# A linear-attention and two-MoE kernel: the diagonals of recurrence step 1 from a second set of scores, and conversion steps in other places

## The chip, the cores and the metric

The kernel runs on one core of a Trainium2 chip. A core has five engines with a queue of instructions each: TensorE (PE: matmuls; PEld: its weight loads), VectorE (DVE), ScalarE (ACT), GpSimd (POOL) and SyncE (SP), which here issues all transfers between memory and the core. Each engine runs its own queue in order and waits where data of another engine is due. The metric is the device time of one execution in microseconds.

## The reference

The inputs are r, k, v (4 batches, 8 heads, 768 positions, head size 48), a decay w and a bonus u for each head and channel, and the weights of two gated blocks. First comes a linear-attention recurrence for each batch and head:

```python
for t in range(S):
    cur = np.einsum('bhd,bhe->bhde', u[None] * kt, vt)
    y[:, :, t] = np.einsum('bhd,bhde->bhe', rt, state + cur)
    state = w[None, :, :, None] * state + np.einsum('bhd,bhe->bhde', kt, vt)
```

Its output, laid out as 3072 tokens of 384 features, goes through `(x @ w_a) * (x @ w_b) @ w_out` (1536 hidden features), and that through `((x @ w1) * (x @ w2)) @ w3 @ w_out` (1024 hidden features). Most weights arrive as 64-bit floats.

## The kernel before, in words

**Recurrence.** The 768 positions are cut into 6 steps of 128. A step and a batch make a unit: units 0 to 3 are step 0, 4 to 7 are step 1, and so on to 23. In a unit the decay is folded into scaled copies of r and k (`prep_r`, `prep_k`, lines 349 to 356: products with the tables tr and tk). `scores` (line 382) multiplies the scaled k with the scaled r into two PSUM tiles "at", one for the even and one for the odd heads; there are two such buffers (pool ps_at). `a_evac` (line 387) copies them to SBUF with the strictly causal mask applied. The diagonal of the scores needs the bonus u and no decay. Units 4 and later compute it apart: `prep_d` (line 358) multiplies r, u and k in their natural layout on GpSimd in two products and sums each head on VectorE into dg, and `a_diag` (line 395) copies dg into the diagonal under the mask ident. Units 0 to 3 have it from a second set of scores with k scaled by u, read from PSUM by `diag_0` (line 402). `y_mm` (line 410) multiplies the state and then the scores into the output tile, `y_evac` (line 447) splits the output into a high and a low part (fp32r, two matmul operands), `s_mm`, `s_decay` and `s_upd` (lines 468 to 500) update the state. The output and the state's increment take the two "at" buffers again.

**Weights.** The class Stream (line 56) takes 27 jobs for the first block, in this order: wab0, wab1, the first part of w_out, wab2, wab3, the second part of w_out, wab4, wab5, the third part of w_out, with three jobs each. A job loads 512 KB of 64-bit floats (line 86; four staging buffers, so a load waits for ScalarE to be done with the job four before it), turns them into 32-bit floats on VectorE (`begin`, lines 101, 117 and 120), casts the high part on ScalarE (`cast`, line 133) and subtracts it on VectorE for the low part (`finish`, line 154). `step` finishes one job and begins the next; `split` forces the jobs that a matmul is about to read.

**First block.** For each tile of 128 hidden features two groups of nine matmuls (line 631: three products of high and low parts, three slices of the depth) fill PSUM tiles "ab"; ScalarE copies one (g, line 650), VectorE multiplies it with the other (line 656), ScalarE casts the product (gh, line 657), VectorE takes its low part (gl, line 662). `m_mm` (lines 684 to 686) multiplies with w_out, two tiles later. The run for step 0 is cut after six tiles (SPLIT), so that the second run, for step 1, can follow.

**Order.** The program writes the order of each queue out by hand. `merge` (line 537) lays three lists into each other: main (the tile groups), side (the recurrence slots of the next step, eight for a unit) and late (conversion steps). In the first run, late spreads 12 or 13 steps evenly.

Of the kernel before, what the change touches and what calls it, by code (L numbers as in the profile page):

```python
# [7 lines left out]
F32 = mybir.dt.float32  # L8
# [12 lines left out]
C = 128  # L21
# [19 lines left out]
STEPS = (1, 1, 1, 0)  # L41
# [5 lines left out]
PRE = 3  # L47

END_0 = 4
LATE = 3  # L50
# [126 lines left out]
def rwkv_moe_kernel(ctx, tc, rkT, nat, wu, wab, wout, w12, w3T, wo2, r_in, k_in, v_in, w_in, u_in, out):  # L177
# [7 lines left out]
    def flat(ap):  # L185
        return ap.rearrange("p a b -> p (a b)")

    with tc.manual_schedule():
# [153 lines left out]
        nc.vector.tensor_tensor(out=wC, in0=pos[:, :, HALF:], in1=pos[:, :, HALF:], op=ALU.mult)  # L342
        s_t = [att.tile([112, NP, 112], F32, name=f"s{b}", bufs=1) for b in range(B)]
# [3 lines left out]
        kf_t, pr_t, y3_t = {}, {}, {}  # L347
# [34 lines left out]
        def scores(u):  # L382
            for x in range(2):
                at_ps[u, x] = ps_at.tile([128, NP, C], F32, name="at")
            scores_f([at_ps[u, x] for x in range(2)], flat(rf_t[u]), kf_t.pop(u))
# [9 lines left out]
        def a_diag(u, hf):  # L395
            d = d_t[u].rearrange("p (q x) -> p x q", x=2)[:, hf, :]
            nc.vector.copy_predicated(
                out=a_t[u][:, 4 * hf:4 * hf + 4, :],
                mask=ident.bitcast(I32).rearrange("p (o n) -> p o n", o=1).to_broadcast([128, 4, C]),
                data=d.rearrange("p (h o) -> p h o", o=1).to_broadcast([128, 4, C]))  # L400

# [100 lines left out]
        def prep_slots(u):  # L502
            return [
                lambda: (prep_r(u, nc.vector), prep_k(u, nc.vector)),
                lambda: prep_d(u, 0),
                lambda: prep_d(u, 1),
                lambda: prep_d(u, 2),
            ]

        def unit_slots(u):  # L510
# [7 lines left out]

            return [
# [72 lines left out]
        for u in range(B):  # L592
# [9 lines left out]
            y_0_evac(u)  # L602
            later_loads(u)
# [9 lines left out]
            for _ in range(STEPS[u]):  # L613
                step()
# [3 lines left out]
        step()  # L618
        for u in range(S_NOW, B):
            k_nat(u)  # L620
        for f in prep_slots(B)[:PRE]:
            f()
        for _ in range(TAIL - 1):
            step()
# [130 lines left out]
        for n, (q, tiles, c) in enumerate(runs):  # L755
# [8 lines left out]
            if n == 0:  # L764
                side = [lambda u=u: (s_mm(u), s_upd(u)) for u in range(S_NOW, B)] + prep_slots(B)[PRE:] + side
            if n == 0:
                late = [step] * (wo_ready[1] - st.begun)
            if n == 1:
                late = [step] * (len(st.jobs) - st.begun + 2)
                late += [lambda: None] * (len(late) // LATE)  # L770
# [359 lines left out]
```

## Time and profile before

| what | before |
|---|---|
| median of 3 runs | 918.27 us (917.95 to 923.23) |
| the profiled execution | 921.02 us, its span 919.2 us |
| mean granted TensorE clock | 0.984 |
| TensorE busy | 889.4 us (97%) |
| VectorE busy | 449.9 us (49%) |
| ScalarE busy | 325.2 us (35%) |
| GpSimd busy | 106.9 us (12%) |

The span goes from the first to the last instruction; the profiled execution's own time is 1.8 us longer, and it is 2.7 us over the median of the runs. The granted clock is the share of full speed that TensorE's clock had in a stretch: 1.0 is 2.4 GHz, 0.5 is 1.2 GHz. A busy time is an average over parts of the program that have different limits, so the table says little of the first 116 us, in which the recurrence's first steps, the conversions and the first tiles run side by side.

### The profile page before, as it was taken

The page shows a single profiled execution, that of the slowest core. Times are in us where ns is not written, and L with a number is a line of the kernel's source. Part 1 is how long each engine was busy: PE and PEld are TensorE (multiplying, and loading weights), DVE is VectorE, ACT ScalarE, POOL GpSimd, SP SyncE. Part 2 cuts the span into 40 slices and gives each one's busy share as a digit, 9 for nine tenths or more (in the row PEclk, how much of TensorE's full clock was granted, in tenths as well). Part 3 has the DMA queues.
Part 4 walks back from the last instruction along what each step waited for, and adds up shares of the span by engine and source line. Part 5 has one row for each costly group of instructions (what it writes and reads, how often), then busy time and mean ns, then how long its engine had stood idle before and what let it go on. Part 6 is the DMA issues. An engine that isn't in the chain of part 4 may idle for free.

```text
span 919.2 us, 12479 instructions
## 1 busy us (share of the span) xinstructions
PE 889.4 (97%) x4962; PEld 754.2 (82%) x4962; DVE 449.9 (49%) x762; ACT 325.2 (35%) x737; POOL 106.9 (12%) x104
## 2 busy tenths in 40 slices
PE   8877999999999999999999999999999999999997
PEld 7665788888888888888888888899988888888886
DVE  8998876356343333433332889566222222223212
ACT  3554565332222232222112778564322222222211
POOL 2204200036033213211100000000000000000000
PEclk9798899999999999999999999999999999999999
DMA  8654531024131221122103555352010101000001
GB/s 263 193 160 138 135 118 63 1 79 154 30 101 46 63 68 59 47 63 81 47 1 109 165 156 172 109 176 71 12 58 11 47 24 47 24 35 1 35 0 38
DMA packets 26065, 73.56 MB, mean 80 GB/s; under 512 B 3152, under 2 KB 7376, under 8 KB 26000
## 3 DMA queue, kind: packets, MB, share of 16 engines
q1 hardware_dynamic: 26000, 72.70, 26.1%
q8 instruction: 41, 0.67, 0.3%
q14 instruction: 24, 0.20, 0.1%
HBM read 61.28 MB, written 9.44 MB: 77 GB/s over the span
## 4 chain that ended last, share of the span: by engine, by line
PE 90%; DVE 6%; issue 1%; DMA 1%; ACT 1%; SPq 0%
PE ab L631 52%; PE m L684 5%; PE m L686 5%; PE m L685 5%; PE at L798 4%; PE o L822 3%; PE o L823 3%; PE o L821 3%; PE at L420 2%; PE at L380 2%; PE at L416 2%; DVE cvt L117 1%; DMA rk<-in_rkT_dram 1%; PE at L823 1%; PE at L821 1%
## 5 line engine op out<-in xcount | busy, mean ns | idle before, releaser
L656 DVE TENSOR_TENSOR ab<-g,ab 128x512 f32<-128x512 f32 x120 | 83.5, 696 | 305.2 <-PE ab L631 272.8
L631 PE MATMUL ab<-xt,w12h 128*128 128x512 f32 x576 | 177.4, 389 | 0.0
L650 ACT COPY g<-ab 128x512 f32<-128x512 f32 x120 | 70.4, 587 | 264.0 <-PE ab L631 263.9
L657 ACT CAST gh<-ab 128x512 fp32r<-128x512 f32 x120 | 70.5, 588 | 253.5 <-DVE ab L656 253.5
L631 PEld LDWEIGHTS ab<-xt,w12h 128*128 128x128 f32 x576 | 107.5, 188 | 18.8
L662 DVE TENSOR_TENSOR gl<-ab,gh 128x512 fp32r<-128x512 f32 x120 | 83.0, 691 | 61.5 <-ACT gh L657 60.8
L631 PE MATMUL ab<-xt,w12l 128*128 128x512 f32 x288 | 112.0, 389 | 0.0
L684 PE MATMUL m<-gh,woh 128*128 128x512 f32 x216 | 85.5, 396 | 0.4 <-ACT woh L133 0.4
L686 PE MATMUL m<-gh,wol 128*128 128x512 f32 x216 | 84.3, 390 | 0.8 <-DVE wol L154 0.8
L685 PE MATMUL m<-gl,woh 128*128 128x512 f32 x216 | 84.3, 390 | 0.0
L631 PEld LDWEIGHTS ab<-xt,w12l 128*128 128x128 f32 x288 | 54.1, 188 | 11.3
L352 POOL TENSOR_TENSOR rk<-rk,tr 112x512 f32<-112x512 f32 x16 | 20.7, 1294 | 281.5 <-DMA rk<-in_rkT_dram 140.3
L631 PE MATMUL ab<-xt,wab0h 128*128 128x512 f32 x144 | 48.0, 415 | 3.1 <-DVE xt L445 2.5
L684 PEld LDWEIGHTS m<-gh,woh 128*128 128x128 f32 x216 | 40.5, 188 | 10.2 <-ACT woh L133 0.8
L686 PEld LDWEIGHTS m<-gh,wol 128*128 128x128 f32 x216 | 40.5, 188 | 9.8 <-DVE wol L154 1.2
L685 PEld LDWEIGHTS m<-gl,woh 128*128 128x128 f32 x216 | 40.6, 188 | 8.3
L631 PE MATMUL ab<-xt,wab1h 128*128 128x512 f32 x144 | 46.9, 408 | 0.0
L631 PE MATMUL ab<-xt,wab4h 128*128 128x512 f32 x144 | 45.5, 397 | 0.0
L631 PE MATMUL ab<-xt,wab3h 128*128 128x512 f32 x144 | 45.5, 397 | 0.0
L631 PE MATMUL ab<-xt,wab2h 128*128 128x512 f32 x144 | 45.4, 397 | 0.0
L631 PE MATMUL ab<-xt,wab5h 128*128 128x512 f32 x144 | 45.0, 394 | 0.0
L117 DVE SCALAR_TENSOR_TENSOR cvt<-stg_t,cvt 128x512 int32<-128x512 int32 x61 | 44.6, 731 | 0.3
(275 smaller groups left out, 1582.2 us busy)
## 6 DMA issues: line engine op xcount, KB each, us to landing
natt<-in_nat_dram SPq DMA_DIRECT2D x20, 576.0 KB, 5.0
rk<-in_rkT_dram SPq DMA_DIRECT2D x24, 448.0 KB, 3.8
stg_t<-in_wab_dram SPq DMA_DIRECT2D x18, 512.0 KB, 4.0
stg_t<-in_w3T_dram SPq DMA_DIRECT2D x16, 512.0 KB, 3.9
stg_t<-in_w_dram SPq DMA_DIRECT2D x12, 512.0 KB, 3.7
stg_t<-in_wout_dram SPq DMA_DIRECT2D x9, 512.0 KB, 3.6
m_d<-m_sb SPq DMA_DIRECT2D x18, 256.0 KB, 3.2
stg_t<-m_d SPq DMA_DIRECT2D x18, 256.0 KB, 2.7
```

The lines of the kernel that those rows point to most:

```text
L117: nc.vector.scalar_tensor_tensor(out=f, in0=w[:, :, 1], scalar=-0x40000000, in1=f, op0=ALU.bitwise_and, op1=ALU.bitwise_or)
L631: mm(ps, lhsT=w[i][:, k, cs], rhs=x[:, j, k, :], start=(n == 0), stop=(n == 3 * KD - 1))
L650: nc.scalar.copy(out=t["g"], in_=t["a"])
L656: nc.vector.tensor_tensor(out=t["b"], in0=g, in1=t["b"], op=ALU.mult)
L657: nc.scalar.copy(out=gh, in_=t["b"])
L662: nc.vector.tensor_tensor(out=gl, in0=t["b"], in1=gh, op=ALU.subtract)
L684: mm(m_ps[q][k], lhsT=wh[:, j, cs], rhs=gh, start=first, stop=False)
L685: mm(m_ps[q][k], lhsT=wh[:, j, cs], rhs=gl, start=False, stop=False)
L686: mm(m_ps[q][k], lhsT=wl[:, j, cs], rhs=gh, start=False, stop=last)
L798: mm(f_ps[i], lhsT=w3_t[i][a][:, g, :], rhs=wo2_t[g // 4][b][:, g % 4, :], start=(n == 0), stop=(n == 3 * NF2 - 1))
L821: mm(o_ps[q][b], lhsT=ph[:, cs], rhs=wh, start=(f == 0), stop=False)
L823: mm(o_ps[q][b], lhsT=pl[:, cs], rhs=wh, start=False, stop=(f == NF2 - 1))
```

## The change

Units 4 to 7 (step 1) no longer use `prep_d`, `a_diag` and dg. A vector uw = u * w (clipped w) is made once. `prep_u` scales the already scaled k of a unit with uw on ScalarE into a tile ku (four activations), and `scores_u` multiplies ku with the scaled r into two more "at" tiles, whose diagonals `diag_0` copies. The decay exponents of the scaled r and k of one position differ by one factor of w, so the product with u * w gives the diagonal without decay. Unit 8 keeps its `prep_d`, in the slots of unit 7.

The conversion steps of the first run are no longer spread by the list late: there is one in the slot of a unit's scores, one in the slot of its `y_mm`, and four at the end of the run. In step 0, steps go ahead of the later loads, and finish, cast and begin are called one by one. In the second run every second place of late holds a step. The order of the jobs is the same.

```diff
--- before.py
+++ after.py
@@ -38,16 +38,13 @@
 
 WARM, WARM_0 = 10, 6
 
-STEPS = (1, 1, 1, 0)
 TAIL = 3
 
 S_NOW = 2
 
 SPLIT = 6
-PRE = 3
 
 END_0 = 4
-LATE = 3
 N_OK = 2 * 128 * N64 + 112 * NP
 
 EXP_LO, EXP_HI = 2.0 ** -15 * 1.125, 2.0 ** 16 * 1.8749
@@ -340,11 +337,13 @@
         nc.vector.tensor_copy(out=tk, in_=tr[:, :, ::-1])
         wC = const.tile([112, NP, 1], F32, name="wC")
         nc.vector.tensor_tensor(out=wC, in0=pos[:, :, HALF:], in1=pos[:, :, HALF:], op=ALU.mult)
+        uw = wc
+        nc.vector.tensor_tensor(out=uw, in0=ut, in1=wc, op=ALU.mult)
         s_t = [att.tile([112, NP, 112], F32, name=f"s{b}", bufs=1) for b in range(B)]
 
         rf_t, d_t, a_t, kn_t, at_ps, xt = {}, {}, {}, {}, {}, {}
 
-        kf_t, pr_t, y3_t = {}, {}, {}
+        kf_t, ku_t, pr_t, y3_t = {}, {}, {}, {}
 
         def prep_r(u, eng):
             r = rk_t[u][:, 0, :]
@@ -382,7 +381,7 @@
         def scores(u):
             for x in range(2):
                 at_ps[u, x] = ps_at.tile([128, NP, C], F32, name="at")
-            scores_f([at_ps[u, x] for x in range(2)], flat(rf_t[u]), kf_t.pop(u))
+            scores_f([at_ps[u, x] for x in range(2)], flat(rf_t[u]), kf_t[u])
 
         def a_evac(u, hf):
             if hf == 0:
@@ -398,6 +397,18 @@
                 out=a_t[u][:, 4 * hf:4 * hf + 4, :],
                 mask=ident.bitcast(I32).rearrange("p (o n) -> p o n", o=1).to_broadcast([128, 4, C]),
                 data=d.rearrange("p (h o) -> p h o", o=1).to_broadcast([128, 4, C]))
+
+        def prep_u(u):
+
+            ku_t[u] = att.tile([112, NP * C], F32, tag="m_part", name="ku", bufs=1)
+            for p in range(NP):
+                s = slice(p * C, (p + 1) * C)
+                nc.scalar.activation(out=ku_t[u][:, s], in_=kf_t[u][:, s], func=ACTF.Copy, scale=uw[:, p:p + 1])
+
+        def scores_u(u):
+            for x in range(2):
+                at_ps["d", u, x] = ps_at.tile([128, NP, C], F32, name="at")
+            scores_f([at_ps["d", u, x] for x in range(2)], flat(rf_t[u]), ku_t.pop(u))
 
         def diag_0(u):
 
@@ -502,9 +513,7 @@
         def prep_slots(u):
             return [
                 lambda: (prep_r(u, nc.vector), prep_k(u, nc.vector)),
-                lambda: prep_d(u, 0),
-                lambda: prep_d(u, 1),
-                lambda: prep_d(u, 2),
+                lambda: prep_u(u),
             ]
 
         def unit_slots(u):
@@ -516,6 +525,18 @@
                 if nxt:
                     f(n, *a)
 
+
+            if u < 2 * B:
+                return [
+                    lambda: (scores(u), after(prep_r, pool), step()),
+                    lambda: (a_evac(u, 0), a_evac(u, 1), after(prep_k, pool)),
+                    lambda: (scores_u(u), k_nat(u)),
+                    lambda: (diag_0(u), n < 2 * B and prep_u(n), n == 2 * B and prep_d(n, 0)),
+                    lambda: (y_mm(u), s_mm(u), step()),
+                    lambda: (load_rk(u + 2), load_nat(u + 2), y_evac(u), (u + 1) % B == 0 and y_shuffle(u // B),
+                             s_decay(u), n == 2 * B and prep_d(n, 1)),
+                    lambda: (s_upd(u), n == 2 * B and prep_d(n, 2)),
+                ]
             return [
                 lambda: (scores(u), after(prep_r, pool)),
                 lambda: (a_evac(u, 0), a_evac(u, 1), after(prep_k, pool)),
@@ -600,6 +621,11 @@
                 both_a(u + 1)
                 diag_0(u + 1)
             y_0_evac(u)
+            if u < 2:
+                step()
+            elif u == 2:
+                st.finish()
+                st.cast()
             later_loads(u)
             if u == 2:
                 tn_ps = ps_m.tile([128, NP, 112], F32, tag="m0", name="tn_ps")
@@ -610,17 +636,18 @@
                     nc.scalar.copy(out=tnat[:, :, x, :], in_=tn_ps[:, :, a:e])
                 for b in range(S_NOW):
                     k_nat(b)
-            for _ in range(STEPS[u]):
-                step()
+                st.finish()
         for u in range(S_NOW):
             s_mm(u)
             s_upd(u)
-        step()
+        st.begin()
+        st.cast()
         for u in range(S_NOW, B):
             k_nat(u)
-        for f in prep_slots(B)[:PRE]:
+        st.finish()
+        for f in prep_slots(B):
             f()
-        for _ in range(TAIL - 1):
+        for _ in range(TAIL):
             step()
 
 
@@ -762,12 +789,12 @@
                     main.append(m_slot(*lag.pop(0)))
             side = step_slots(c) if c else []
             if n == 0:
-                side = [lambda u=u: (s_mm(u), s_upd(u)) for u in range(S_NOW, B)] + prep_slots(B)[PRE:] + side
+                side = [lambda u=u: (s_mm(u), s_upd(u)) for u in range(S_NOW, B)] + side
             if n == 0:
-                late = [step] * (wo_ready[1] - st.begun)
+                late = [lambda: None] * (len(main) - END_0) + [step] * END_0
             if n == 1:
-                late = [step] * (len(st.jobs) - st.begun + 2)
-                late += [lambda: None] * (len(late) // LATE)
+                late = [step] * 2 + [step, lambda: None] * (len(st.jobs) - st.begun)
+                late += [lambda: None] * (len(main) - len(late))
             if q == NB - 1:
                 for i in range(4):
                     add_w12(i)
```

The order on two engines, before and then changed. VectorE, from the state update of unit 4 (s) to the diagonal of unit 5 (a_sc); cvt is a conversion, wol the low half of w_out's first part, gl a low half of the gated product:

```order
L498 TENSOR_TENSOR s_168<-at,s_168 48x4x48 x2
L366 TENSOR_REDUCE dg<-pr 128x8
L656 TENSOR_TENSOR ab<-g,ab 128x512
L154 TENSOR_TENSOR wol_617<-cvt,woh_616 128x512
L117 SCALAR_TENSOR_TENSOR cvt<-stg_t,cvt 128x512
L101 TENSOR_SCALAR cvt<-stg_t 128x512
L120 SCALAR_TENSOR_TENSOR cvt<-stg_t,cvt 128x512
L662 TENSOR_TENSOR gl<-ab,gh 128x512
L352 TENSOR_TENSOR rk<-rk,tr 112x512
L391 TENSOR_TENSOR a_sc<-at,mask 128x512 x2
L356 TENSOR_TENSOR rk<-rk,tk 112x512
L397 COPY_PREDICATED a_sc<-ident,dg 128x512 x2
```

```order
L509 TENSOR_TENSOR s_169<-at,s_169 48x4x48 x2
L351 TENSOR_TENSOR rk<-rk,tr 112x512
L151 TENSOR_TENSOR wol_629<-cvt,woh_628 128x512
L114 SCALAR_TENSOR_TENSOR cvt<-stg_t,cvt 128x512
L98 TENSOR_SCALAR cvt<-stg_t 128x512
L117 SCALAR_TENSOR_TENSOR cvt<-stg_t,cvt 128x512
L683 TENSOR_TENSOR ab<-g,ab 128x512
L689 TENSOR_TENSOR gl<-ab,gh 128x512
L390 TENSOR_TENSOR a_sc<-at,mask 128x512 x2
L355 TENSOR_TENSOR rk<-rk,tk 112x512
L372 TENSOR_TENSOR kn<-natt,tnat 128x384
L416 COPY_PREDICATED a_sc<-ident,at 128x512 x2
```

The reduction dg is gone; the r product of unit 6 (rk with tr) stands directly behind the state update, and the low half and the conversion stand ahead of the gated product; the natural k product (kn) and the key product are now between the masks and the diagonal, which reads "at" in place of dg.

SyncE, from the natural k of step 0 (k_96) to the load of w_out's first part; stg_t are the conversions' loads, rk and natt the loads of units 4 and 5:

```order
L291 DMA k_96<-in_nat_dram 128x384 x4
L86 DMA stg_t<-in_wab_dram 128x512 x2
L214 DMA rk<-in_rkT_dram 112x1024
L294 DMA u_bc<-in_u_dram 128x384
L223 DMA natt<-in_nat_dram 128x1152
L86 DMA stg_t<-in_wab_dram 128x512
L214 DMA rk<-in_rkT_dram 112x1024
L223 DMA natt<-in_nat_dram 128x1152
L86 DMA stg_t<-in_wout_dram 128x512 x3
```

```order
L288 DMA k_96<-in_nat_dram 128x384 x4
L83 DMA stg_t<-in_wab_dram 128x512 x2
L211 DMA rk<-in_rkT_dram 112x1024
L291 DMA u_bc<-in_u_dram 128x384
L220 DMA natt<-in_nat_dram 128x1152
L211 DMA rk<-in_rkT_dram 112x1024
L220 DMA natt<-in_nat_dram 128x1152
L83 DMA stg_t<-in_wout_dram 128x512 x3
```

The single load of wab between units 4 and 5 now stands ahead of unit 4's loads (the fourth one has moved ahead of k_96, so two remain behind it). On TensorE, the new 8 scores stand behind nine matmuls after the first 8 in units 5 to 7, and directly behind them in unit 4.

## Rows read from the trace of the kernel before

**Rows 1.** stretches: us, busy PE PEld DVE ACT POOL, granted clock, DMA, GB/s

```profile
0.00:28.30 28.30, 24.16 (x264) 21.36 (x264) 24.36 (x51) 10.46 (x29) 6.36 (x19) 0.94 0.86 259
...
28.30:99.99 71.69, 54.01 (x400) 42.38 (x397) 62.15 (x107) 37.70 (x101) 17.32 (x13) 0.83 0.51 153
...
50.00:53.20 3.20, 3.18 (x33) 2.67 (x33) 3.17 (x6) 2.02 (x8) 0.00 (x0) 0.50 0.80 196
...
116.09:919.20 803.11, 796.28 (x4240) 678.80 (x4238) 347.47 (x584) 267.07 (x585) 76.68 (x67) 1.00 0.22 66
```

**Rows 2.** TensorE's waits: us in total, times, longest

```profile
PE ab L631 <- DVE wab2l L154: 5.8, 2, 3.6
...
PE at L420 <- DVE a_sc L397: 4.2, 3, 2.8
...
PE at L380 <- DVE s L498: 3.1, 1, 3.1
```

**Rows 3.** timeline, TensorE: start us, us, engine, line, operation, idle before

```profile
57.51 1.16 PE L380 MATMUL at<-rk 48*128 48x128 f32 x16
...
58.60 0.73 PE L631 MATMUL ab<-xt,wab1h 128*128 128x512 f32 x2
...
60.78 1.04 PE L416 MATMUL at<-rk,s 112*112 112x128 f32 x8
...
70.85 2.04 PE L380 MATMUL at<-rk 48*128 48x128 f32 x14 [3.15 <-DVE s L498]
...
80.00 1.08 PE L420 MATMUL at<-a_sc,natt 128*48 128x128 f32 x16
...
114.40 0.50 PE L686 MATMUL m<-gh,wol 128*128 128x512 f32 x1 [0.76 <-DVE wol L154]
```

**Rows 4.** timeline, VectorE

```profile
25.40 1.34 DVE L405 COPY_PREDICATED a<-ident,d_ps 128x512 f32<-128x512 int32 x2
...
29.17 1.49 DVE L117 SCALAR_TENSOR_TENSOR cvt<-stg_t,cvt 128x512 int32<-128x512 int32 x1
...
33.39 0.68 DVE L117 SCALAR_TENSOR_TENSOR cvt<-stg_t,cvt 128x512 int32<-128x512 int32 x1
...
34.93 1.02 DVE L373 TENSOR_TENSOR k<-k,tnat 128x384 f32<-128x384 f32 x2
...
41.35 0.55 DVE L366 TENSOR_REDUCE dg<-pr 128x8 f32<-128x384 f32 x1
...
49.24 1.35 DVE L397 COPY_PREDICATED a_sc<-ident,dg 128x512 f32<-128x512 int32 x2
...
54.42 0.72 DVE L498 TENSOR_TENSOR s<-at,s 48x192 f32<-48x192 f32 x2 [0.36 <-ACT s L488]
...
99.27 0.72 DVE L498 TENSOR_TENSOR s<-at,s 48x192 f32<-48x192 f32 x2 [0.36 <-ACT s L488]
...
103.53 2.49 DVE L101 TENSOR_SCALAR cvt<-stg_t 128x512 int32<-128x512 int32 x1
...
113.67 0.68 DVE L154 TENSOR_TENSOR wol<-cvt,woh 128x512 fp32r<-128x512 f32 x1
```

**Rows 5.** groups by line, VectorE, 28.3-100 us: count, busy us, mean ns

```profile
L356 DVE TENSOR_TENSOR rk<-rk,tk 112x512 f32<-112x512 f32 x4 | 4.0, 1002 | 0.0
...
L352 DVE TENSOR_TENSOR rk<-rk,tr 112x512 f32<-112x512 f32 x4 | 2.7, 683 | 0.0
```

**Rows 6.** groups by line, GpSimd, 28.3 to 85 us

```profile
L361 POOL TENSOR_TENSOR pr<-natt,u_bc 128x384 f32<-128x384 f32 x4 | 6.6, 1654 | 45.4 <-DMA natt<-in_nat_dram 25.3 <-DVE dg L366 20.1
...
L363 POOL TENSOR_TENSOR pr<-pr,natt 128x384 f32<-128x384 f32 x4 | 4.3, 1078 | 0.3
```

**Rows 7.** timeline, ScalarE

```profile
98.01 1.23 ACT L488 ACTIVATE s<-s,wC 112x112 f32<-112x112 f32 x4
```

**Rows 8.** DMA issues at 51.85 and 61.85 us: KB, us from issue to landing

```profile
rk<-in_rkT_dram SPq DMA_DIRECT2D x1, 448.0 KB, 6.3
...
rk<-in_rkT_dram SPq DMA_DIRECT2D x1, 448.0 KB, 3.5
```

## The prediction

> **What bounds the kernel now.** I read the busy time by stretches first. From 116.1 us to the end TensorE works 796.28 of 803.11 us at the full granted clock; from 28.3 to 100.0 us (the recurrence's step 1 and the first feature tiles) it works 54.01 of 71.69 us at a mean granted clock of 0.83, and there VectorE is the busiest, 62.15 of 71.69 [rows 1]. The change edits only this head, so whatever it brings is a shift of the moment at which TensorE leaves it. Then TensorE's waits: those of weight are for VectorE, 5.8 us for the low half of a converted weight (wab2l), 4.2 us for the masked scores a_sc, 3.1 us for the state update s [rows 2]. The timeline shows what a wait costs beside its own length: the scores' 16 matmul records take 1.16 us, yet 14 of them take 2.04 us after the wait of 3.15 us [rows 3], and the granted clock is 0.50 (1.2 GHz) in the 3.2 us behind the wait of 2.8 us [rows 1, 2]. So the reader is to see a head in which VectorE's queue sets the pace and TensorE's clock falls after each longer wait. The head's last gate is the low half of w_out's second part: TensorE waits for it up to 114.40 us [rows 3]; VectorE starts it at 113.67 us, 14.4 us after the last unit's state update at 99.27 us [rows 4].
>
> **What the change removes.** For units 4 to 7 the products on GpSimd and their sum on VectorE go. The sums are four reductions of 0.55 us, 2.2 us of VectorE's queue [rows 4]. The eight products (6.6 + 4.3 = 10.9 us on GpSimd, [rows 6]) ran beside VectorE and stretched it: the conversion's L117 took 1.49 us at 29.17 us where 0.68 us is usual [rows 4], 0.8 us more, and the instruction behind it as much; the key product L356 takes 1.00 us on average and its twin L352 0.68, 4 x 0.32 = 1.3 us [rows 5]. That is 2.9 us. Together VectorE's queue gets 5.1 us shorter.
>
> The Trainium skill, page "SBUF — State Buffer", has a stronger rule: a VectorE instruction with two SBUF inputs and a GpSimd instruction that reads SBUF share a port pair, held exclusively for a whole instruction, so that the second blocks fully. By that rule up to all 10.9 us of the products could come back, where the rows give 2.9; I take the rows, and the rule is the fourth rival.
>
> **What it adds.** Each of the four units gets a second set of 8 scores on TensorE: by the first set, 57.51 to 58.60, 1.1 us at full clock, 4.4 us in all; about twice that at half clock [rows 3]. They fall into time in which TensorE waits anyway. Four ScalarE copies a unit make the scaled keys; four of nearly their size take 1.23 us [rows 7], on an engine that is half idle in this stretch (37.70 of 71.69 us, [rows 1]); if that cover went, the second scores would wait for them. The diagonal's masked copy reads PSUM instead of SBUF: 1.34 us for two against 1.35 [rows 4], nothing. The one tiny product for u*w lies in the wait for the first loads: nothing.
>
> **What it moves.** The conversions ahead of the last state update are as many in both orders: 12 finished, 14 begun. A step (1.54 us, 33.39 to 34.93 us [rows 4], and 0.6 for its low half) now stands between the scores and their masking, another between the diagonal and the output's eviction. So they cost VectorE nothing in total; what counts is the round trip. Both score sets share two PSUM buffers: the second set waits for the masking, the diagonal for the second set, the output for the diagonal. That is one more pass from TensorE to VectorE and back in each unit.
>
> One unit at full clock, from state update to state update: VectorE runs the next unit's r product 0.6, a low half 0.6, the step 1.54, the gated product 0.6, waits 0.65 for a ScalarE cast, its low half 0.6 (4.6 in all), then the masks 1.2; the second scores end 0.6 later; TensorE runs nine w1 matmuls 2.2 (58.60 to 60.78), the state's part 1.0 and the scores' part 0.9 [rows 3]; ScalarE evicts 0.55 and decays the state 1.23 [rows 7]; the update takes 0.75 [rows 4]. The sum is 13.0 us. Before, the updates lay 15.0 us apart on average (99.27 less 54.42, by three, [rows 4]).
>
> Two waits are new, both on transfers. SyncE's queue now has the sixth conversion's load ahead of unit 4's r and k, and it waits for a ScalarE read near 28.4 us; behind it stand unit 4's and 5's loads and then the seventh conversion's. VectorE then comes to unit 4's r and k some 0.6 us early, and to the seventh load 0 to 1.2 us early (2.8 MB stand ahead, and the head's rate is 259 GB/s, [rows 1]); I take 0.6. And unit 6's r product now comes right behind unit 4's state update, while its load can be issued only after unit 4's state matmuls, near 51.7 us. That load took 6.3 us before, the next unit's 3.5 [rows 8]. It lands at 55.2 to 58.0 and VectorE is there at 55.0: a wait of 0.2 to 3.0 us, taken as 2.2, nearer to the row of the same load, with everything on VectorE, unit 5's masking first, queued behind it.
>
> The Trainium skill, page "DMA: Bandwidth & Descriptors", section "Queues, rings and completion order", says that each DMA engine consumes a queue's descriptors in ring order. That speaks against this edit, since it puts the seventh load behind all five; by it the full 1.2 us would be lost, 0.6 more than in my sum.
>
> **The sum.** Up to the end of unit 4's masking VectorE's queue is 18.4 us of work and waits from 27.1 us on, 45.5 (45.3 before): five steps stand ahead of it. TensorE, with its scores done by 40.5, waits over 4 us there, its clock falls, and unit 4's update ends near 55.0, as before (55.1). Then 3 x 13.0 = 39.0, plus 2.2 for unit 6's load, plus 2.8 of half clock in unit 5 (its second scores wait some 4 us for a masking that stands behind that load): 99.0 against 100.0 us, 1.0 us gained. The 14.4 us up to w_out's low half stay: the same instructions in the same order, and GpSimd's next products stretch them as before (2.49 us for L101 at 103.53 us, [rows 4]). TensorE now arrives some 4 us early at that gate and waits; its clock may fall, 0 to 2.3 us lost (some 5 us at half speed), taken as 1.1. Net 0.1 us lost: nothing to be measured. The profiled execution's 921.0 us become 921.1, and against the median of the runs, 2.7 us lower, **918.4**. The ends of the unknowns put this case between 914.7 and 921.0. About 1%, 9.2 us, is what a measurement tells from no change.
>
> **Rivals.** *The loop closes up* (0.24): unit 6's load lands in time and the clock holds; 55.0 + 39.0 = 94.0, 6.0 us gained, 1.1 given back at the gate: 913.5. If the conversions up to the gate then also miss GpSimd's next products (4.2 us of stretch there, of which 2.1 at 103.53), 909.3. For it: VectorE's queue is 5.1 us shorter; against: every unit has one more round trip. *Slower, the clock stays down through the units* (0.14): 4.6 us of VectorE's work stand between an update and the masking, and TensorE has only its scores and nine matmuls, 3.3 us, to do meanwhile. In units 6 and 7 I count waits of 1.9 and 1.3 us ahead of the scores; where one reaches the 2.8 us after which the clock was seen down, the unit's nine matmuls, state and scores' part take twice their 4.1 us: 922.5 for one unit, 926.6 for two, 928 with what is left of unit 5. *TensorE is freed* (0.03): VectorE's idle 9.5 us of the stretch [rows 1] go with the 5.1: 903.8. *The port rule in full* (0.05): 8.0 us more than my 2.9 come back: 910.4. For none of these 0.02. The change can hardly fail to do what it says: the order shows both score sets and no reductions.
>
> **Numbers.** Forecast 0.52, 914.7 to 921.0. The range 909 to 925 adds the loop that closes up and one unit at half clock. Faster by over 1%: the freed TensorE, a third of the first rival, a little of the port rule, 0.12; slower by over 1%: a third of the slow rival, 0.05; the rest 0.83.
>
> **What would show it.** Right: TensorE's waits for wab2l mostly gone, but one of over 3 us for a_sc ahead of unit 4's second scores; VectorE waiting for unit 6's r and k; unit 7's update at 98 to 100 us; a wait of 3 to 4 us for w_out's second part near 112 us. Wrong: that update at 94 us or earlier and no wait for the load; or a granted clock of 0.5 through units 5 to 7; or TensorE leaving the head without a wait for w_out.

## The result: 1.2% slower, outside the range

The changed kernel took 932.98 us (median of 4 runs, 929.10 to 933.94), the kernel before 918.32 us beside it: a ratio of 1.0121, 95% interval 1.0087 to 1.0155. Measured again later beside the kernels below it took 928.26 us against 920.33, ratio 1.0086 (1.0061 to 1.0112). The forecast was 918.4 us, the range 909 to 925, and slower by over 1% had a chance of 0.05. The ratios leave out a few slow runs: one of e13 below (1772 us), and two each of the kernel before beside e1 to e4 and beside e13 to e16.

### The profile page after: what moved, and what is told of

It reads as the page before. It is cut to its first block, busy times and chain, and to the rows that moved or that the text cites. A ratio compares the mean times of both kernels' runs of the same rounds, so it can differ in the third digit from the quotient of the medians.

```text
span 930.9 us, 12618 instructions
## 1 busy us (share of the span) xinstructions
PE 894.3 (96%) x5026; PEld 757.8 (81%) x5026; DVE 444.2 (48%) x759; ACT 329.4 (35%) x753; POOL 94.9 (10%) x96
## 4 chain that ended last, share of the span: by engine, by line
PE 89%; DVE 4%; DMA 4%; ACT 2%; issue 1%; SPq 0%; DVEq 0%
PE ab L658 51%; PE m L711 5%; PE m L712 5%; PE m L713 5%; PE at L825 4%; PE at L379 3%; PE o L849 3%; PE o L850 3%; PE o L848 3%; PE at L431 2%; DMA rk<-in_rkT_dram 2%; PE at L427 2%; DMA stg_t<-in_wout_dram 1%; PE at L850 1%; PE at L848 1%
## 5 line engine op out<-in xcount | busy, mean ns | idle before, releaser
L658 PE MATMUL ab<-xt,w12h 128*128 128x512 f32 x576 | 177.4, 389 | 0.0
L658 PEld LDWEIGHTS ab<-xt,w12h 128*128 128x128 f32 x576 | 107.5, 188 | 18.8
L658 PE MATMUL ab<-xt,w12l 128*128 128x512 f32 x288 | 112.1, 389 | 0.0
L713 PE MATMUL m<-gh,wol 128*128 128x512 f32 x216 | 84.3, 390 | 0.8 <-DVE wol L151 0.8
L658 PEld LDWEIGHTS ab<-xt,w12l 128*128 128x128 f32 x288 | 54.1, 188 | 11.3
L713 PEld LDWEIGHTS m<-gh,wol 128*128 128x128 f32 x216 | 40.5, 188 | 9.8 <-DVE wol L151 1.2
L658 PE MATMUL ab<-xt,wab0h 128*128 128x512 f32 x144 | 47.1, 408 | 0.7 <-ACT wab0h L130 0.7
L658 PE MATMUL ab<-xt,wab2h 128*128 128x512 f32 x144 | 46.8, 407 | 0.0
L658 PE MATMUL ab<-xt,wab1h 128*128 128x512 f32 x144 | 46.5, 405 | 0.0
L658 PE MATMUL ab<-xt,wab4h 128*128 128x512 f32 x144 | 45.5, 397 | 0.0
L658 PE MATMUL ab<-xt,wab3h 128*128 128x512 f32 x144 | 45.5, 397 | 0.0
L658 PE MATMUL ab<-xt,wab5h 128*128 128x512 f32 x144 | 45.0, 394 | 0.0
L153 ACT ACTIVATE sq<-sq,small 128x512 bf16<-128x512 bf16 x61 | 44.3, 725 | 0.3
```

The lines of the kernel that those rows point to most:

```text
L153: nc.scalar.activation(out=sq, in_=sq, func=ACTF.Sign, bias=self.small, accum_out=self.chk[:, n, 1:2])
L658: mm(ps, lhsT=w[i][:, k, cs], rhs=x[:, j, k, :], start=(n == 0), stop=(n == 3 * KD - 1))
L713: mm(m_ps[q][k], lhsT=wl[:, j, cs], rhs=gh, start=False, stop=last)
```

## The profile after

The profiled execution took 932.83 us, span 930.9 us, mean granted clock 0.983. The stretches of [rows 1], with the same columns:

```profile
0.00:28.30 28.30, 23.40 (x236) 20.71 (x237) 23.59 (x50) 9.46 (x25) 6.01 (x19) 0.88 0.75 215
28.30:99.99 71.69, 50.07 (x424) 39.40 (x423) 54.30 (x96) 39.91 (x110) 5.19 (x5) 0.88 0.52 157
116.09:919.20 803.11, 799.63 (x4246) 679.92 (x4245) 355.81 (x597) 272.19 (x600) 79.07 (x69) 1.00 0.21 66
```

VectorE's busy time from 28.3 to 100 us fell from 62.15 to 54.30 us, so the removal is there; TensorE's fell too, from 54.01 to 50.07 us. It did less in this stretch, not more. TensorE's waits (those of [rows 2]; L379 is the scores, L658 the feature tiles, L713 w_out's low half):

```profile
PE at L379 <- DVE a_sc L390: 13.7, 2, 9.9
PE ab L658 <- DVE wab2l L151: 3.7, 1, 3.7
...
PE at L379 <- DVE s L509: 2.9, 2, 1.8
...
PE m L713 <- DVE wol L151: 0.8, 1, 0.8
```

The 13.7 us are new: the second scores wait for VectorE to have masked the first, 9.9 us in unit 4 and 3.8 in unit 5. TensorE's timeline at these places, and at unit 7 and the gate (columns: start us, us, engine, line, operation, out<-in, shape, in brackets the idle time before and what ended it):

```profile
50.22 2.58 PE L379 MATMUL at<-rk,ku 48*128 48x128 f32 x16 [9.88 <-DVE a_sc L390]
...
68.26 2.17 PE L379 MATMUL at<-rk,ku 48*128 48x128 f32 x16 [3.82 <-DVE a_sc L390]
70.36 1.22 PE L658 MATMUL ab<-xt,wab1h 128*128 128x512 f32 x2
...
73.59 1.04 PE L427 MATMUL at<-rk,s 112*112 112x128 f32 x8
...
100.30 0.79 PE L658 MATMUL ab<-xt,wab2l 128*128 128x512 f32 x1 [3.69 <-DVE wab2l L151]
101.03 2.08 PE L379 MATMUL at<-rk,ku 48*128 48x128 f32 x16
...
125.18 0.50 PE L713 MATMUL m<-gh,wol 128*128 128x512 f32 x1 [0.76 <-DVE wol L151]
```

The second scores take 2.1 to 2.6 us there instead of 1.1, and two feature matmuls 1.22 instead of 0.62: half clock after each of the three waits. In unit 5 the matmuls of the state's part (L427) start only at 73.59 us, behind the second scores and nine feature matmuls. The gate stands at 125.18 us, 10.8 us later than the 114.40 of [rows 3]. VectorE's timeline, where [rows 4] were (L509 is the state update):

```profile
45.70 0.43 DVE L98 TENSOR_SCALAR cvt<-stg_t 128x512 int32<-128x512 int32 x1 [4.64 <-DMA stg_t<-in_wout_dram]
...
60.17 0.72 DVE L509 TENSOR_TENSOR s<-at,s 48x192 f32<-48x192 f32 x2 [0.42 <-issue]
62.61 0.69 DVE L351 TENSOR_TENSOR rk<-rk,tr 112x512 f32<-112x512 f32 x1 [1.72 <-DMA rk<-in_rkT_dram]
...
76.37 0.29 DVE L469 TENSOR_TENSOR y<-at,y 112x128 fp32r<-112x128 f32 x1 [2.84 <-ACT xt L468]
...
79.58 0.72 DVE L509 TENSOR_TENSOR s<-at,s 48x192 f32<-48x192 f32 x2
...
92.58 0.71 DVE L509 TENSOR_TENSOR s<-at,s 48x192 f32<-48x192 f32 x2
...
94.88 3.02 DVE L117 SCALAR_TENSOR_TENSOR cvt<-stg_t,cvt 128x512 int32<-128x512 int32 x1
97.92 1.29 DVE L390 TENSOR_TENSOR a_sc<-at,mask 128x512 f32<-128x512 f32 x2
...
103.14 1.34 DVE L416 COPY_PREDICATED a_sc<-ident,at 128x512 f32<-128x512 int32 x2 [2.89 <-PE at L379]
...
111.23 0.72 DVE L509 TENSOR_TENSOR s<-at,s 48x192 f32<-48x192 f32 x2 [0.77 <-issue]
...
124.45 0.68 DVE L151 TENSOR_TENSOR wol<-cvt,woh 128x512 fp32r<-128x512 f32 x1
```

The four updates stand at 60.17, 79.58, 92.58 and 111.23 us, so the loops are 19.4, 13.0 and 18.7 us. In unit 5 VectorE itself stands idle for 2.84 us ahead of the output's low part (L469), which comes behind those matmuls. Before, the two updates that [rows 4] leave out were

```profile
69.99 0.72 DVE L498 TENSOR_TENSOR s<-at,s 48x192 f32<-48x192 f32 x2
...
82.92 0.72 DVE L498 TENSOR_TENSOR s<-at,s 48x192 f32<-48x192 f32 x2 [0.36 <-ACT s L488]
```

so its loops were 15.6, 12.9 and 16.3 us. Two places lie off the forecast: the load of the seventh conversion is waited for 4.64 us and unit 4's update comes 5.7 us later than before; and in unit 7 a conversion takes 3.02 us instead of 0.68. GpSimd's products for unit 8 begin beside that conversion:

```profile
94.72 1.39 POOL L351 TENSOR_TENSOR rk<-rk,tr 112x512 f32<-112x512 f32 x1 [75.32 <-ACT sq L153]
...
99.78 1.32 POOL L362 TENSOR_TENSOR pr<-pr,natt 128x384 f32<-128x384 f32 x1
```

And the transfers issued from 32.0 to 36.0 us (KB, us from issue to landing): the seventh conversion's load stands behind the four loads of units 4 and 5.

```profile
natt<-in_nat_dram SPq DMA_DIRECT2D x1, 576.0 KB, 12.2
stg_t<-in_wout_dram SPq DMA_DIRECT2D x1, 512.0 KB, 10.2
rk<-in_rkT_dram SPq DMA_DIRECT2D x1, 448.0 KB, 10.7
```

## The experiments

Each stood beside the kernel before, which took 920.3 to 921.0 us, but on four chips: e1 to e4 on one, a0, e5, e6 and e8 on a second, e9 to e12 on a third, e13 to e16 on a fourth. So ratios are compared, not times. Differences in us are ratio less one, times 920.5; by the intervals a difference of two rows is good to some 2 to 4 us (my estimate). Three theories stood at the start. Theory 1, mine: the loss is the transfers put ahead and GpSimd's products for unit 8 beside unit 7's masking. Theory 2: the second scores' round trip itself. Theory 3: the conversion steps between scores and masking.

| kernel | median us | ratio (95%) | us |
|---|---|---|---|
| a0_change_again | 928.26 | 1.0086 (1.0061 to 1.0112) | +7.9 |
| e1_loads_first | 924.02 | 1.0032 (1.0014 to 1.0050) | +2.9 |
| e2_scores_only | 930.29 | 1.0095 (1.0074 to 1.0115) | +8.7 |
| e3_moves_only | 926.57 | 1.0057 (1.0037 to 1.0076) | +5.2 |
| e4_unit8_late | 921.66 | 1.0010 (0.9990 to 1.0031) | +0.9 |
| e5_loads_and_unit8 | 919.11 | 0.9988 (0.9973 to 1.0003) | -1.1 |
| e6_mask_first | 917.53 | 0.9967 (0.9948 to 0.9985) | -3.0 |
| e8_before_unit8_late | 913.51 | 0.9929 (0.9905 to 0.9953) | -6.5 |
| e9_scores_unit8 | 925.52 | 1.0049 (1.0033 to 1.0066) | +4.5 |
| e10_keep_busy | 916.99 | 0.9959 (0.9944 to 0.9974) | -3.8 |
| e11_moves_unit8 | 914.25 | 0.9927 (0.9903 to 0.9950) | -6.7 |
| e12_r_behind_mask | 914.38 | 0.9929 (0.9906 to 0.9952) | -6.5 |
| e13_sixth_load | 926.33 | 1.0054 (1.0035 to 1.0073) | +5.0 |
| e14_fourth_load | 928.41 | 1.0102 (1.0063 to 1.0141) | +9.4 |
| e15_mask_first_only | 922.54 | 1.0022 (1.0007 to 1.0038) | +2.0 |
| e16_mask_first_busy | 915.89 | 0.9959 (0.9940 to 0.9977) | -3.8 |

### The change again

> The changed kernel itself once more, to stand on the same chip as the others. All theories: 929 to 935, 1.0 to 1.5% above the kernel before.

At 928.3 us just under the expected interval. Its profiled execution, the fastest of its six runs (924.66 us), had a granted clock of 1.00 in the first 28.3 us (the start clock, from here on), where the recorded one had 0.88. Its four updates on VectorE:

```profile
54.76 0.72 DVE L509 TENSOR_TENSOR s<-at,s 48x192 f32<-48x192 f32 x2 [0.42 <-issue]
...
73.91 0.72 DVE L509 TENSOR_TENSOR s<-at,s 48x192 f32<-48x192 f32 x2
...
86.93 0.71 DVE L509 TENSOR_TENSOR s<-at,s 48x192 f32<-48x192 f32 x2
...
102.45 0.72 DVE L509 TENSOR_TENSOR s<-at,s 48x192 f32<-48x192 f32 x2 [0.77 <-issue]
```

Unit 4's update lies 5.4 us earlier than in the recorded execution of the same program, so one profile does not price the head; the medians do.

### The order of the loads

```diff
# e1: in step 0's loop
+            later_loads(u)
             if u < 2:
                 step()
             elif u == 2:
                 st.finish()
                 st.cast()
-            later_loads(u)
# e13: this for u == 2 alone; e14: this for u == 0 alone
```

> The changed kernel, with only SyncE's order in the first four units put back: the loads for the four keys of step 0 stand ahead of the fourth conversion's load, and unit 4's r, k, natural tile ahead of the sixth conversion's load; every other engine's program is the same. Theory 1 (the loss lies in transfers put ahead and in GpSimd's products for unit 8): xt(2) on VectorE is back near 26.6 us (28.1), the seventh conversion's load wait shrinks from 4.64 to under 2 us, unit 4's state update moves from 60.2 to 55 to 57 us; unit 7's loop keeps its 18 us; the time is 4 to 6 us below the changed kernel, 927 to 929. Theory 2 (the second scores' round trip itself): unit 4's update stays within 1.5 us of 60.2, time 931 to 933. Theory 3 (conversion steps between scores and masking): as theory 2, 931 to 933.

5.0 us below the change, as theory 1 had it, though at 924 us and not 927 to 929, since the change itself ran 5 us faster in the second measurement. In its profile nothing waits for the seventh load, while unit 5's loop is still 19.4 us. The profiled execution is the slowest of e1's twelve runs (929.97 us), so it is set beside one of the same start clock: the recorded change and e1 both had 0.88. SyncE comes to unit 4's r and k, in the change and in e1, at

```profile
30.35 0.42 SPq L211 DMA_DIRECT2D rk<-in_rkT_dram  x1
```

```profile
19.69 0.43 SPq L211 DMA_DIRECT2D rk<-in_rkT_dram  x1
```

since in the change the sixth conversion's load ahead of it waits for a staging buffer. Unit 4's update is at 60.17 us in the change (58.47 in e4, which has the same loads and start clock), and in e1 and in e13, both with 0.88, at

```profile
54.74 0.72 DVE L509 TENSOR_TENSOR s<-at,s 48x192 f32<-48x192 f32 x2 [0.42 <-issue]
```

```profile
54.68 0.72 DVE L509 TENSOR_TENSOR s<-at,s 48x192 f32<-48x192 f32 x2 [0.42 <-issue]
```

> The changed kernel with the sixth conversion's load behind unit 4's loads again; the fourth conversion's load stays ahead of the keys of step 0. If the sixth load is the cause (unit 4's r and k and the seventh conversion's load come late behind it): 923.5 to 925, 3.5 to 5 us below the change, and the seventh load's wait of 2.7 to 4.6 us falls under 1 us. If the fourth load is: 927 to 929, as the change.

> The changed kernel with the fourth conversion's load behind the keys of step 0 again; the sixth conversion's load stays ahead of unit 4's loads. If the sixth load is the cause: 926.5 to 929, at most 1.5 us below the change, the seventh load still waited for by 2 us or more. If the fourth load is (unit 2's r and k land later, all of step 0 starts 1.5 us late): 923 to 925.

The sixth conversion's load put back alone gains 2.9 us, less than the 3.5 expected; the fourth's alone nothing (+1.5, inside the intervals), and its profile still waits 3.29 us for the seventh load. By unit 4's update the sixth load is the whole of it; the 2.1 us between the medians of e13 and e1 lie inside the intervals.

### The second scores and the moved steps, each alone

```diff
# e2: before, with for units 4 to 7 (steps and loads where they were)
-    lambda: (a_diag(u, 0), a_diag(u, 1), k_nat(u)),
-    lambda: after(prep_d, 0),
+    lambda: (scores_u(u), k_nat(u)),
+    lambda: (diag_0(u), prep_u(n) if n < 2 * B else prep_d(n, 0)),
     ...   # prep_d(4, ...) gives way to prep_u(4) too
# e3: the change, with
-    lambda: (scores_u(u), k_nat(u)),
-    lambda: (diag_0(u), n < 2 * B and prep_u(n), n == 2 * B and prep_d(n, 0)),
+    lambda: k_nat(u),
+    lambda: (a_diag(u, 0), a_diag(u, 1), after(prep_d, 0)),
     ...   # prep_d's other two parts in the last two slots
```

> The kernel before with only the diagonal's source changed for units 4 to 7 (scaled keys by ScalarE, second scores, masked copy from PSUM; no GpSimd product and no reduction for these units), all conversion steps and loads where they were before. Theory 1: VectorE's queue is 5.1 us shorter and the round trip is covered, so the last state update is 0 to 5 us earlier than before's 99.3 us and the time is 913 to 919. Theory 2 (the round trip itself costs): each of four units loses 2 to 3 us, the time is 926 to 932. Theory 3: no loss without the moves, 913 to 919, as theory 1.

> The changed kernel with the diagonals of units 4 to 7 made as before (GpSimd's products, VectorE's reduction, masked copy from SBUF), but the conversion steps, the loads' order and the seven slots a unit as in the change. Theory 1: the seventh load's wait (4 to 5 us) and unit 7's delay stay, and GpSimd's products come back beside VectorE: 931 to 938. Theory 2 (the round trip is the loss): 917 to 922. Theory 3 (the moved steps are the loss): 930 to 936, with the masking late in every unit, loops of over 15 us in units 5 and 6 too.

e2 lost 8.7 us: theory 1, mine, was wrong in its main point, and the second scores cost by themselves. e3 hit no theory's interval: its 5.2 us agree with the 5.0 that e1 gave back for the loads, whose order e3 shares with the change. From e3 to the change the second scores are 2.7 us more, by itself inside the intervals.

### Unit 8's work out of unit 7

```diff
# e4: the change; e8: the kernel before; both with
-    load_rk(u + 2), load_nat(u + 2)   # for u = 6, 7
-    after(prep_r), after(prep_k), after(prep_d, ...)   # for n = 8
+    # in the second run's side list
+    (load_rk(8), load_nat(8), load_rk(9), load_nat(9)),
+    (prep_r(8, g), prep_k(8, g)), prep_d(8, 0), prep_d(8, 1), ..., prep_d(8, 2)
```

> The changed kernel, with the loads of units 8 and 9 and all of unit 8's preparation (r and k products, diagonal products, their reduction) taken out of unit 7's slots and put beside the next run of feature tiles, so that GpSimd has nothing but unit 7's key product there. Theory 1: the conversion beside them (3.02 us at 94.88 us) is back at 0.7 us, unit 7's masking comes 4 to 5 us earlier, no half clock there, unit 7's loop is 13 us instead of 18.65 and the gate at w_out's second part 5 to 8 us earlier (117 to 120 us): 925 to 928. Theories 2 and 3: the loop of unit 7 keeps 17 us or more, the time is 931 to 934.

> The kernel before, with unit 8's and 9's loads and unit 8's preparation put beside the next run as in e4_unit8_late; nothing of the change. Theory 1 in its strict form (GpSimd's products for unit 8 hurt only where the second scores queue behind a wait for VectorE's low halves): 918 to 921, within 0.2% of before. Rival (they stretch VectorE's conversions in both kernels): unit 7's loop falls from 16.4 to 13 us and the gate comes 4 to 7 us earlier, 914 to 917; then what e4 gained is no property of the change.

e4 gained 7.0 us over the change, as theory 1 expected (5 to 8 below the first measurement), and unit 7's loop was 13.3 us. Yet e8 gained 6.5 us in the kernel before, half a us beyond the rival's interval for that run, and unit 7's loop there fell from 16.3 to 13.1 us, so the rival holds: GpSimd's work for unit 8 stretches VectorE in both kernels, and it is no part of the loss. The edit moves the loads of units 8 and 9 as well; no run takes these from the products. In the kernel before, VectorE beside those products:

```profile
88.36 1.50 DVE L117 SCALAR_TENSOR_TENSOR cvt<-stg_t,cvt 128x512 int32<-128x512 int32 x1
89.78 1.21 DVE L101 TENSOR_SCALAR cvt<-stg_t 128x512 int32<-128x512 int32 x1
```

and in e8, without them:

```profile
88.90 0.68 DVE L117 SCALAR_TENSOR_TENSOR cvt<-stg_t,cvt 128x512 int32<-128x512 int32 x1
89.50 0.42 DVE L101 TENSOR_SCALAR cvt<-stg_t 128x512 int32<-128x512 int32 x1
```

Each of the two takes twice its time or more beside a product.

> The changed kernel with both edits: SyncE's order of the first units put back (as in e1_loads_first) and unit 8's loads and preparation beside the next run (as in e4_unit8_late). Theory 1 (these two hold the loss, apart from each other): unit 4's update at 54.7 us, unit 7's loop 13.3 us, w_out's second part near 108 to 114 us; the two measured gains, 8.2 and 10.3 us against the change's 11.1 us of loss, add up: 913 to 916. Rival (they overlap: what one gives back the other, or TensorE's half clock in units 5 and 6, takes): 918 to 922, no better than the better of the two alone.

With both edits the two gains did not quite add up: 5.0 and 7.0 us would be 12.0, and e5 gained 9.0 over the change (from +7.9 to -1.1). The fair comparison is e8 and e11, and against these e5 is still 5.4 and 5.6 us slow.

### What the second scores cost, and why

With unit 8's work gone, the same two halves again:

```diff
# e9: e8 with e2's edit (second scores, steps in before's places)
# e11: e8 with e3's edit (steps moved, diagonals as before), loads as before
```

> e2_scores_only (before's places for the steps and loads, second scores for the diagonals) with unit 8's loads and preparation beside the next run: against e8_before_unit8_late only the diagonal's source differs. Theory A (the second scores cost by themselves: TensorE must wait for the masking, its clock falls, unit 5 takes 19 to 21 us instead of 15.6): 918 to 922, 5 to 8 us above e8's 913.5. Theory B (they cost only where GpSimd's products for unit 8 stretch the low half that stands ahead of them, unit 7): 912 to 915, at most 1.5 us above e8.

> e3_moves_only (the moved conversion steps, diagonals by GpSimd's products and VectorE's reduction) with the loads' order put back and unit 8's preparation beside the next run: against e8_before_unit8_late only the places of the conversion steps differ. If the moved steps alone cost (theory 3): 917 to 921. If they are free, as the prediction had it: 912 to 915.

e9 stands 11.0 us above e8: theory A, by more than it said. e11 is level with e8 (0.9927 and 0.9929): the moved steps cost nothing that the intervals, some 3 us, would show. e5 differs from e11 in the diagonals alone and is 5.6 us slower, so with the steps in the change's places the second scores cost about half of what they cost in the old ones. In e9, unit 5, TensorE's and VectorE's timelines:

```profile
61.02 2.58 PE L382 MATMUL at<-rk,ku 48*128 48x128 f32 x16 [1.79 <-DVE a_sc L393]
63.52 1.22 PE L657 MATMUL ab<-xt,wab1h 128*128 128x512 f32 x2
```

```profile
54.32 0.72 DVE L512 TENSOR_TENSOR s<-at,s 48x192 f32<-48x192 f32 x2 [0.41 <-issue]
...
75.26 0.72 DVE L512 TENSOR_TENSOR s<-at,s 48x192 f32<-48x192 f32 x2
```

A wait of only 1.8 us, then half clock through the scores and the feature matmuls, and a loop of 20.9 us. Three edits then went at that wait:

```diff
# e6: e5 with step() behind the masking; e12, shown: the r product behind it too
-    lambda: (scores(u), prep_r(n, pool), step()),
-    lambda: (a_evac(u, 0), a_evac(u, 1), prep_k(n, pool)),
+    lambda: scores(u),
+    lambda: (a_evac(u, 0), a_evac(u, 1), prep_r(n, pool), prep_k(n, pool), step()),
# e10: e5, with 14 (u = 4) and 12 (u = 5) matmuls into an unread bank
+    for _ in range(KEEP[u]): mm(t, lhsT=ident, rhs=ident, start=True, stop=True)
     scores_u(u)
```

> e5_loads_and_unit8 with one more edit: in each unit the conversion step that stands between the scores and their masking is put behind the masking. Theory 3 (that step is what keeps TensorE waiting ahead of the second scores and drops its clock): the waits for a_sc at the second scores fall from 8.7 and 2.4 us to under 1 us beyond unit 4, units 5 and 6 take 13 us or less at full clock instead of 19.4 and 16, 4 to 9 us below e5. Theory 1: VectorE's queue is as long, only its order changes; within 2 us of e5.

> e6_mask_first with the next unit's r product on VectorE behind the masking too, so that unit 5's masking no longer stands behind the wait for unit 6's load (2.88 us there). If that wait and the half clock behind it are what is left of the loss: unit 5 takes 13 to 15 us instead of 18.5, the last state update 3 to 5 us earlier, 913 to 915, even with e8. If the gain is taken back at w_out's second part or by other waits of TensorE: 916 to 918, as e6.

> e5_loads_and_unit8 with 14 and 12 extra matmuls of 128 columns on TensorE (into a bank that nothing reads) ahead of the second scores of units 4 and 5, where it waits 5.1 and 3.1 us. Theory A (the half clock behind these waits is the price): the second scores and the feature matmuls behind them keep full clock, unit 5 takes 15 to 16 us instead of 18.7, 2 to 5 us below e5's 919.1: 914 to 917. Rival (the round trip's wait is the price, the clock follows it but costs nothing more, since VectorE sets the pace): within 1 us of e5, 918.5 to 920.

e6 gained 1.9 us, inside theory 1's 2 us and inside the intervals, and kept a unit 5 of 18.5 us: the masking stood behind a wait of 2.88 us for unit 6's r and k. e12 takes it out of that wait. There the second scores of unit 5 follow the feature matmuls with no wait:

```profile
56.15 1.16 PE L379 MATMUL at<-rk,ku 48*128 48x128 f32 x16
```

and the loop is 14.6 us:

```profile
51.96 0.72 DVE L509 TENSOR_TENSOR s<-at,s 48x192 f32<-48x192 f32 x2 [0.42 <-issue]
...
66.56 0.72 DVE L509 TENSOR_TENSOR s<-at,s 48x192 f32<-48x192 f32 x2
```

Units 6 and 7 take 14.4 and 13.6 us, 2.0 us more than in e5, so part of the gain in unit 5 goes again. At 0.9929 e12 equals e11, which has the old diagonals: with the masking first and unit 8's work away the second scores cost nothing that the intervals would show, and they gain nothing either. The four ScalarE copies a unit, which come with them in every pair, are in e12 too, so they are not the price. Whether more than two "at" buffers would spare the second scores the wait, no run shows. e10 kept e5's waits but filled them; the granted clock from 28.3 to 99.99 us, 0.93 in e5, is full (columns as in [rows 1]):

```profile
28.30:99.99 71.69, 61.82 (x545) 49.68 (x542) 56.08 (x105) 42.80 (x119) 1.02 (x1) 1.00 0.45 135
```

That gained 2.7 us, theory A, of the 5.6 at stake. Up to unit 4's update e10 is e1 with those matmuls, and both had a start clock of 0.88; the update, at 54.74 us in e1, is 2.4 us earlier. Unit 5's loop stayed at 18.5 us and not 15 to 16, but there VectorE waited longer for unit 6's r and k, in e10 and then in e5:

```profile
52.35 0.72 DVE L510 TENSOR_TENSOR s<-at,s 48x192 f32<-48x192 f32 x2 [0.42 <-issue]
55.40 0.69 DVE L352 TENSOR_TENSOR rk<-rk,tr 112x512 f32<-112x512 f32 x1 [2.33 <-DMA rk<-in_rkT_dram]
```

```profile
53.46 0.69 DVE L351 TENSOR_TENSOR rk<-rk,tr 112x512 f32<-112x512 f32 x1 [0.98 <-DMA rk<-in_rkT_dram]
```

From this product to unit 5's update it is 15.4 us in e10 (update at 70.82) and 17.0 in e5 (70.43). So by the medians the half clock is about half the price; the rest is put down to the late masking itself, which e12 takes away together with the half clock in unit 5. Unit 4 shows the two apart, one execution each: e12 keeps a wait and the half clock there,

```profile
41.02 2.58 PE L379 MATMUL at<-rk,ku 48*128 48x128 f32 x16 [2.39 <-DVE a_sc L390]
```

and its update at 51.96 us is still 2.8 us ahead of e1's, at the same start clock.

> The changed kernel with the loads' order put back, and the masking of each unit ahead of the conversion step and of the next unit's r product; unit 8's work stays where the change has it. If late masking is the rest of the loss: 1.5 to 4 us below e1_loads_first (ratio 1.0032), so 919 to 922, level with the kernel before. If unit 8's products undo it (unit 7 waits as in the change): 923 to 925.

e15 is e1 with e12's edit, unit 8's work in its old place. It gained 0.9 us, inside the intervals, instead of 1.5 to 4: units 5 and 6 take 14.6 and 14.4 us as in e12, but unit 7 takes 19.8 us, since its second scores stand behind a low half that GpSimd stretches, and the diagonal waits for them:

```profile
84.11 2.46 DVE L151 TENSOR_TENSOR wab2l<-cvt,wab2h 128x512 fp32r<-128x512 f32 x1
...
94.01 1.34 DVE L416 COPY_PREDICATED a_sc<-ident,at 128x512 f32<-128x512 int32 x2 [2.89 <-PE at L379]
```

> e12_r_behind_mask (ratio 0.9929) with 10 extra matmuls on TensorE, into a bank that nothing reads, in the wait of 2.4 us ahead of unit 4's second scores. If the half clock behind that wait (7 us of matmuls at twice their length) costs on the path: 1 to 3 us below e12, 911 to 913.5. If VectorE's queue sets the end there: within 1 us of e12, 913.5 to 915.5.

e16 (e12 with 10 such matmuls ahead of unit 4's second scores) missed on the other side, 2.8 us above e12, about what the intervals leave open; unit 4's update, at the same start clock of 0.88, stands at 53.68 us for 51.96. The wait only moved on: TensorE now came early to the diagonal, and the half clock fell on the state's and scores' part, which hold the update.

```profile
48.12 2.05 PE L428 MATMUL at<-rk,s 112*112 112x128 f32 x8 [2.97 <-DVE a_sc L417]
```

## Why the prediction was wrong, step by step

- **VectorE's queue 5.1 us shorter:** right; its busy time over the whole span fell by 5.7 us (449.9 to 444.2). It bought nothing: e9's VectorE is busy 2.0 us less than e8's over the span (442.9 to 444.9) and e9 is 11.0 us slower, so the queue's length did not set the pace.
- **The second scores "fall into time in which TensorE waits anyway":** this step failed. They do not fill a wait, they make one: TensorE runs in order, so its feature matmuls, and behind them the state's part that the update needs, stand behind scores that wait for a masking. e11 to e5 and e8 to e9 put it at 5.6 and 11.0 us; in the change it is the 2.9 us that e1 leaves (2.7 from e3 to a0). The sum saw the waits in units 4 and 5, but had nothing for the first and 2.8 us of half clock for the second.
- **The moved steps cost VectorE nothing:** right as far as the intervals reach (e8 to e11, 0.2 us).
- **The seventh load, 0.6 us:** this term failed too, and in the change it is the larger part. The mechanism was right, the size wrong by nearly eight times: the wait was 4.64 us (2.73 in a0), and the order of the loads costs 5.0 us, most of it with the sixth load (e13). I let the loads start near 28.4 us; SyncE reached unit 4's r and k at 30.35, and the load landed 10.2 us after its issue, in e1 4.4. The Trainium skill's rule in "DMA: Bandwidth & Descriptors" (section "Queues, rings and completion order"), that each engine works through a queue's descriptors in ring order, pointed this way; the 1.2 us that I drew from it were too few as well.
- **Unit 4's update near 55.0 us:** 60.17 in the recorded execution, 54.76 in a0's, with a full start clock. With the loads put back it is 54.7 at the recorded start clock and 51.76 at a full one (e5), so the order of the loads is what moved it.
- **The wait for unit 6's r and k, 0.2 to 3.0 us, taken as 2.2:** right; 1.72 us here, 0.45 to 2.88 in the variants.
- **The loop of 13.0 us:** right where nothing disturbs it; unit 6 took 13.00 and, in a0, 13.02 us. But it took 12.9 before as well: the average of 15.0 that the sum set 13.0 against hid 15.6, 12.9 and 16.3. Unit 5 took 19.4 and 19.2 instead of 18.0.
- **Unit 7 at 13.0 us:** wrong, 18.7 and 15.5. GpSimd's products for unit 8 were put behind the last update only. They cost the kernel before as much (e8), whose unit 7 took 16.3 us, so they explain where the recorded time stands, and little of why it differs: 2.3 us more in the recorded execution, 0.8 less in a0's.
- **The 14.4 us to w_out's low half:** 13.2 us here (111.23 to 124.45); the granted clock from 100 to 130 us was 0.89.
- **The signs:** of those for being right, the wait for a_sc ahead of unit 4's second scores (9.88 us) and the wait for unit 6's r and k came. Unit 7's update at 98 to 100 us (111.23) and the wait of 3 to 4 us for w_out's second part (0.76) did not.

Between the two profiled executions, before and changed (start clocks 0.94 and 0.88), the gate's 10.8 us divide by the updates into 5.8 up to unit 4's, 3.8 in unit 5, 0.1 in unit 6, 2.3 in unit 7, and 1.2 given back from there to w_out's low half. By the medians, the 7.9 us of the second measurement are 5.0 for the loads and 2.9 that e1 leaves for the second scores. The second is a remainder, but e3, with the loads' order and without the second scores, lost 5.2 us, which agrees. The slow rival (0.14) had part of the mechanism, the clock down behind waits ahead of the scores, but in units 6 and 7 and without the loads; the recorded 933 us lie beyond its 928. Why the first measurement lost 12.1 per mille and the second 8.6 stays open; the intervals overlap.

The port rule of the Trainium skill, page "SBUF — State Buffer" (section "SBUF: two separate sides"), my fourth rival, has the loser block for the whole of the other's instruction. The rows show part of that: five products, four for unit 8 and unit 7's natural k, take 6.5 us on GpSimd in the kernel before, and the four instructions beside them there take 5.3 us, in e8 2.5: 2.9 more. VectorE's masking, which reads a score from PSUM, kept its 1.29 us beside a product (97.92 us in the profile after), as that rule's condition of two SBUF inputs has it; but L101, with one SBUF input, went from 0.42 to 1.21 us. The same section of the Trainium skill counts instructions in a two-port mode too; whether L101 runs in one, no row shows.

The three fastest versions, e8, e11 and e12, are level at 0.993 of the time before. None owes it to the change: what gains is unit 8's work and the loads of units 8 and 9 out of unit 7.

## What to carry to other kernels

A dependent matmul that goes into the queue of an engine with other work is not free because that engine has idle time: count what stands behind it, and where the instruction that releases it stands in the other engine's queue. Before adding it, put the releasing instruction first there; with unit 8's work out of unit 7 that took the price from 5.6 us to nothing measurable here (e5, e12); with it in unit 7 it gained 0.9 us (e15), inside the intervals. And in a list of loads in one queue, price each one that is moved back with the whole traffic now ahead of it.

## What the runs showed of the hardware

- The first 28.3 us of one and the same program ran at a mean granted clock of 0.88 in one execution and 1.00 in another (the change and its repeat), and unit 4's update stood 5.4 us apart.
- Idle TensorE time filled with unread matmuls held the granted clock at 1.00 from 28.3 to 99.99 us (e10), but filling one wait of several let the clock fall at the next (e16).
- A VectorE conversion of 0.68 us took up to 3.02 us beside GpSimd's products.
